# Four floats of padding between the q and k rows of an mLSTM and feed-forward kernel

## The chip, the cores and the metric

The kernel runs on one core of a Trainium2 chip. The metric is device time in microseconds for one execution, from three executions of the kernel before; lower is better. The engines are TensorE (PE, with its weight loads shown as PEld), VectorE (DVE), ScalarE (ACT), GpSimd (POOL) and SyncE (SP). SP computes nothing here; its queue issues nearly all transfers between the chip's memory (HBM) and the on-chip buffer (SBUF). Sixteen DMA engines carry them.

## The reference

There are 4 batches of 8 heads, 768 time steps, head width 40. Each of the 32 chains of (batch, head) runs an mLSTM recurrence, and its gated output feeds a feed-forward layer of 320 to 2048 to 320 with a softplus between.

```python
for t in range(S):
    m_new = np.maximum(f_gate[:, :, t] + m, i_gate[:, :, t])
    f_stab = np.exp(f_gate[:, :, t] + m - m_new)
    i_stab = np.exp(i_gate[:, :, t] - m_new)
    C = f_stab * C + i_stab * einsum('bhd,bhe->bhde', vt, kt)     # broadcast over d, e
    n = f_stab * n + i_stab * kt
    h_tilde = einsum('bhde,bhe->bhd', C, qt)
    denom = np.maximum(np.abs(einsum('bhd,bhd->bh', n, qt)), 1.0)
    y[:, :, t] = sigmoid(o_gate[:, :, t]) * h_tilde / denom
x = y.transpose(0, 2, 1, 3).reshape(B * S, H * D)                 # 3072 x 320
out = softplus(x @ w_in) @ w_out
```

## The kernel before, in words

The sequence is cut into 24 steps (one batch, 128 tokens, all 8 heads). A step `z` loads q and k of its 8 heads into one tile `qk`, and v and k by token into `vt`. It computes score products of k and q (`scores`, L463), weighs them by decays (`by_decays`), adds the part that comes from the carried state (`states`, `values`), normalises and gates the result, and writes it as columns of a tile `X`. Three steps make one `X` of 384 tokens; eight of them go through the feed-forward products: `hp` (L974, eight matmuls of 128x384 for each of 16 slices of the hidden layer) and `po` (L937, nine matmuls of 128x320 for each slice). The feed-forward weights are split into a high and a low part as they are loaded, so that the products stay exact enough.

Before the first `hp` there is a front of some 37 us: the first gates are read and scanned, three steps run one after another, and a few matmuls of the identity (`keep_warm`, L731) are placed between them. After it the feed-forward products run on PE without a break and the steps of later tiles are laid between them. The order of the work on every engine is written out: each piece of a step has a due time in a table (`WHEN`) counted in matmuls, and a context `in_order` ties each instruction to the one before it on its engine. So an instruction that waits holds up all that stands behind it on its engine, and SP is such an engine too: its loads are issued in the fixed order of the program.

A transfer also waits, ahead of its issue, for the transfer that last used its completion counter; there are eight such counters for SP, handed out in turn.

The q and k of a step lie in `qk[z.s]` in HBM as 2 halves x 40 rows (head dimension) x 2 (q, k) x 512 floats (4 heads of 128 tokens), built on the host. In SBUF each half takes 40 partitions, starting at partition 0 and 64 (`PP` is 64). Each step issues two loads `qk<-in_qk` (L382), one for each half, and one load `vt<-in_vk` (L385). The tile `qk` has three buffers.

`fc0` holds the running product of the first tokens' forget gates; it is written at L170, read by a matmul at L175 and by a small copy, all in the front. The single buffer with the tag `sig` in pool `p1` is used by the gate load of step 3 (L754) and, from step 6 on, by the tile `nw` of each step (L679).

Of the kernel before, what the change touches and what calls it, by code (L numbers as in the profile page):

```python
# [8 lines left out]
F32 = mybir.dt.float32  # L9
# [8 lines left out]
B, H, S, D = 4, 8, 768, 40  # L18
L = 128
# [4 lines left out]
HG = H // 2  # L24
# [7 lines left out]
NCHAIN = B * H  # L32
PP = 64
# [3 lines left out]
FIRST = [(1, 0), (2, 0), (0, 0), (3, 0)]  # L37
ORDER = FIRST + [(b, c) for b in range(B) for c in range(NC) if (b, c) not in FIRST]
NI = 3


@with_exitstack
def mlstm_moe_kernel(
# [11 lines left out]
    nc = tc.nc  # L55
# [7 lines left out]
    cpool = ctx.enter_context(tc.tile_pool(name="cpool", bufs=1))  # L63
    p1 = ctx.enter_context(tc.tile_pool(name="p1", bufs=1))
    p2 = ctx.enter_context(tc.tile_pool(name="p2", bufs=2))
# [30 lines left out]
    fc_d = dpool.tile([NC, NCHAIN, L], F32, name="fc_d")  # L96
    fl_d = [dpool.tile([2, 2, B, 2, NI, NQ], F32, name=f"fl_d{k}") for k in range(2)]
    flast = [cpool.tile([128, 2, B, 2, NI, NQ], F32, name=f"flast{k}") for k in range(2)]
    fl_s = cpool.tile([NCHAIN, NC, NQ], F32, name="fl_s")
    gT = cpool.tile([128, NC, NQ, B, HG], F32, name="gT")  # L100
    fcT = cpool.tile([128, NI, B, H], F32, name="fcT")
    y1z = cpool.tile([128, 2, 4, E], F32, name="y1z")
    nc.gpsimd.memset(y1z[0:Q], 0.0)
    m_end = cpool.tile([NCHAIN, 2], F32, name="m_end")
    fc0 = cpool.tile([NCHAIN, L], F32, name="fc0")

    g0 = cpool.tile([128, 2, L], F32, name="g0")
    fg0 = g0[:, 0]
# [73 lines left out]
    def later_gates(part):  # L182

        c0, c1 = ((1, NI), (NI, NC))[part]
        n, w = c1 - c0, (c1 - c0) * L
# [28 lines left out]
        yield  # L214
        fd, p0 = fl_d[part], part * NI
        nc.sync.dma_start(
# [160 lines left out]

    def load(z):

        z.qk = p2.tile([128, 2, HG, L], F32, tag="qk", bufs=3, name=f"qk{z.n}")  # L380
        for x in range(2):
            nc.sync.dma_start(z.qk[x * PP : x * PP + D], qk[z.s, x])  # L382
        z.q, z.k = z.qk[:, 0], z.qk[:, 1]
        z.vt = p2.tile([128, VW + DM], F32, tag="vt", bufs=3, name=f"vt{z.n}")
        nc.sync.dma_start(z.vt, vk[z.s])  # L385
        z.v1 = z.vt[:, 0:VW].rearrange("p (q j e) -> p q j e", q=NQ, j=HG)
        z.kt = z.vt[:, VW:]
# [124 lines left out]
    def fl(z, q):  # L512
        return flast[z.c // NI][0 : PP + D, :, z.b, :, z.c % NI, q]

# [316 lines left out]
    def plain_step(z, times):  # L831
        spare = z.s in (1, 2)
        fs = dict(
            load=load, fb=decays, scan=decay, vi=gate_values, vw=state_values, sig=out_gate,
            ga=plain_scores, pm=by_decays, st=states, cp=keep_states, old=decay_old,
            mid=mid_state, new=new_state, gc=lambda z: values(z, z.s in SPARE_C), sum=sum_values, nrm=norm, sg=scale_gate, x=gated,
            xp=turn_x, xh=high_x, xl=low_x,
        )
        for (name, f), t in zip(fs.items(), times, strict=True):
            once(f"{name}{z.s}", t, event, name, f, z)  # L840
# [3 lines left out]
    def wide_step(z, base, after):  # L844
        d = 18 + 30 * (z.s == NH)
        g = after - base
        for name, f, t in (
            ("fb", decays, -64), ("load", load, -48), ("scan", decay, -8), ("vw", state_values, 2), ("old", decay_old, 6),
            ("ga", group, 14), ("pm", by_decays, 17), ("cp", keep_states, 17), ("vi", gate_values, 20), ("mid", mid_state, 24),
            ("new", new_state, 30), ("fc", load_decays, g - 34),  # L850
        ) + ((("gc", values_wide, g),) if z.s == NS - 1 else ()) + (
            ("ym", scale_wide, g + 5), ("ya", add_wide, g + 5), ("yd", write_wide, g + 8), ("rd", read_wide, g + 42),
            ("fin", finish_wide, g + 91 + d), ("end", end_wide, g + 92 + d), ("xh", high_wide, g + 95 + d),
            ("xl", low_wide, g + 98 + d),
        ):
            once(f"{name}{z.s}" if z.s < 9 else name, base + t, event, name, f, z, base=base)
# [328 lines left out]
```

## Time and profile before

| | |
|---|---|
| Median of 3 runs | 438.4 us (436.66, 438.4, 439.52) |
| Profiled execution | span 438.4 us; the page gives no other time for it |
| PE busy | 427.3 us, 97% of the span |
| DVE, ACT, POOL busy | 253.6, 214.5, 106.1 us |
| Mean granted TensorE clock | 0.977 of full |
| Moved by DMA | 55.93 MB, mean 128 GB/s |
| Loads of q and k | 48, of 160 KB each |

A span is the time from the first to the last instruction of the core. An engine is busy when it executes, so 97% on PE says that little of the span is left without PE work, and the places where PE stands idle are the ones to look for. The granted clock is 1.0 at 2.4 GHz and 0.5 at 1.2 GHz; stretches at 0.5 lie in the first 36 us. DMA share is the mean busy share of the 16 DMA engines.

### The profile page before, as it was taken

How to read it: one execution, taken by the hardware profiler on the slowest of the kernel's cores; microseconds unless marked ns; L12 is line 12 of the kernel's file. 1: busy time of each engine (PE TensorE's matmuls, PEld its weight loads, DVE VectorE, ACT ScalarE, POOL GpSimd, SP SyncE). 2: the span in 40 equal slices, each digit the busy share in tenths (PEclk: the TensorE clock that was granted, in tenths of full speed). 3: DMA queues.
4: the chain of work that ended last, by engine and by line, in shares of the span. 5: the costliest groups of instructions: out<-in, count | busy, mean ns of one | idle time of the engine just before them, and what ended most of it. 6: DMA issues, size and time to landing. Idle time of an engine off the chain costs nothing.

```text
span 438.4 us, 12718 instructions
## 1 busy us (share of the span) xinstructions
PE 427.3 (97%) x5302; PEld 414.3 (95%) x5302; DVE 253.6 (58%) x479; ACT 214.5 (49%) x445; POOL 106.1 (24%) x171
## 2 busy tenths in 40 slices
PE   7869999999999999999999999999999999999997
PEld 6758999999999999999999999999999999999996
DVE  6678998677866556456465556466365554422221
ACT  5388898768347333534236333544336333333332
POOL 3425334545454302111132202121122200000000
PEclk9568999999999999999999999999999999999999
DMA  7877886776376373544463263553553331001001
GB/s 197 263 218 206 234 256 178 222 197 182 82 171 182 95 192 75 135 125 104 116 179 107 59 163 94 151 125 84 135 164 88 99 95 36 0 1 46 1 0 46
DMA packets 52089, 55.93 MB, mean 128 GB/s; under 512 B 5664, under 2 KB 42176, under 8 KB 52032
## 3 DMA queue, kind: packets, MB, share of 16 engines
q1 hardware_dynamic: 49008, 51.68, 43.1%
q10 hardware_dynamic: 3024, 3.44, 2.3%
q8 instruction: 41, 0.67, 0.6%
q14 instruction: 16, 0.13, 0.1%
HBM read 46.47 MB, written 8.64 MB: 126 GB/s over the span
## 4 chain that ended last, share of the span: by engine, by line
PE 95%; DMA 3%; issue 1%; ACT 0%; DVE 0%; SPq 0%
PE hp L974 41%; PE po L937 40%; PE ga L463 3%; PE gc L652 2%; PE gc L640 2%; PE ga L480 2%; PE po L731 2%; DMA qk<-in_qk 2%; DMA wr<-in_w_in 1%; PE xp L709 1%; PE gc L579 1%; PE gc L587 1%; PE xp L707 1%; PE gb L463 1%; PE gb L480 0%
## 5 line engine op out<-in xcount | busy, mean ns | idle before, releaser
L974 PE MATMUL hp<-X,wih 128*128 128x384 f32 x768 | 175.3, 337 | 0.0
L862 ACT ACTIVATE gh<-hp 128x384 fp32r<-128x384 f32 x128 | 63.0, 492 | 168.0 <-PE hp L974 140.6
L866 DVE TENSOR_TENSOR gl<-hp,gh 128x384 fp32r<-128x384 f32 x128 | 70.7, 555 | 123.1 <-ACT hp L863 122.8
L974 PEld LDWEIGHTS hp<-X,wih 128*128 128x128 f32 x768 | 133.3, 188 | 0.3 <-issue 0.2
L937 PE MATMUL po<-woh,gl 128*128 128x320 f32 x384 | 83.2, 313 | 0.0
L937 PE MATMUL po<-woh,gh 128*128 128x320 f32 x384 | 80.7, 310 | 0.0
L937 PE MATMUL po<-wol,gh 128*128 128x320 f32 x384 | 80.7, 310 | 0.0
L937 PEld LDWEIGHTS po<-woh,gh 128*128 128x128 f32 x384 | 65.8, 188 | 0.2
L974 PE MATMUL hp<-X,wil 128*128 128x384 f32 x256 | 65.7, 337 | 0.0
L937 PEld LDWEIGHTS po<-woh,gl 128*128 128x128 f32 x384 | 62.3, 188 | 0.9 <-issue 0.2
L937 PEld LDWEIGHTS po<-wol,gh 128*128 128x128 f32 x384 | 62.1, 188 | 0.8 <-issue 0.3
L863 ACT ACTIVATE hp<-hp 128x384 f32<-128x384 f32 x128 | 62.4, 487 | 0.0
L974 PEld LDWEIGHTS hp<-X,wil 128*128 128x128 f32 x256 | 46.1, 188 | 0.1
L426 POOL TENSOR_TENSOR vw<-vt,gw 128x328 f32<-128x328 f32 x22 | 17.4, 790 | 118.4 <-DVE gw L417 105.3
L412 DVE TENSOR_TENSOR_SCAN pw<-fb,ident 128x512 f32<-128x512 f32 x24 | 30.1, 1256 | 0.0
L426 POOL TENSOR_TENSOR values_in<-vt,gT 128x328 f32<-128x328 f32 x18 | 13.3, 739 | 67.7 <-PE gc L652 63.9
L463 PEld LDWEIGHTS ga<-qk 40*64 40x64 f32 x448 | 13.2, 134 | 5.5 <-issue 3.9
L558 POOL TENSOR_TENSOR c<-c,cp 104x164 f32<-104x164 f32 x20 | 14.1, 703 | 15.0 <-DVE c L426 13.7
L463 PE MATMUL ga<-qk 40*64 40x64 f32 x448 | 16.6, 224 | 1.1 <-DMA qk<-in_qk 1.1
L685 DVE RECIPROCAL nm<-nm 128x128 f32<-128x128 f32 x18 | 17.2, 953 | 0.6
L480 PE MATMUL ga<-vw,vt 64*40 64x41 f32 (+1 forms) x416 | 14.2, 222 | 2.3 <-issue 2.3
L426 POOL TENSOR_TENSOR c<-c,flast 104x164 f32<-104x164 f32 x33 | 15.6, 473 | 1.0
(159 smaller groups left out, 477.6 us busy)
## 6 DMA issues: line engine op xcount, KB each, us to landing
vt<-in_vk SPq DMA_DIRECT2D x24, 324.0 KB
qk<-in_qk SPq DMA_DIRECT2D x48, 160.0 KB
fb<-fz_d SPq DMA_DIRECT2D x42, 128.0 KB
wo<-in_w_out SPq DMA_DIRECT2D x8, 640.0 KB
wr<-in_w_in SPq DMA_DIRECT2D x8, 512.0 KB
eg<-in_oT SPq DMA_DIRECT2D x6, 576.0 KB
yd<-y SPq DMA_DIRECT2D x36, 96.0 KB
out<-ob ACTq DMA_DIRECT2D x21, 160.0 KB
```

The source lines that it names most:

```text
L412: nc.vector.tensor_tensor_scan(z.pw.rearrange(flat), z.fb.rearrange(flat), ident4.rearrange(flat), 0.0, ALU.mult, ALU.add)
L426: e.tensor_tensor(to, of, by.unsqueeze(3).broadcast_to([to.shape[0], a, b, w]), op=ALU.mult)
L463: nc.tensor.matmul(z.ga[x][y * Q : (y + 1) * Q, (i * NQ + q) * Q : (i * NQ + q + 1) * Q], z.k[rows, g, ts], z.q[rows, g, ts], start=True, ...
L480: nc.tensor.matmul(z.ga[y][x * PP : x * PP + w, c0 : c0 + E], z.kt[y * Q : (y + 1) * Q, j * D : j * D + w], z.vw[y * Q : (y + 1) * Q, q, x ...
L558: nc.gpsimd.tensor_tensor(heads(c), heads(c), z.cp[:, :, 1], op=ALU.add)
L640: nc.tensor.matmul(gc[out, x, c0 : c0 + Q], (z.cm if q else z.old)[rows, g * E : g * E + w], z.q[rows, g, q * Q : (q + 1) * Q], start=True ...
L685: nc.vector.reciprocal(nm, nm)
L862: nc.scalar.activation(gh, hp, AF.Softplus)
L863: nc.scalar.activation(hp, hp, AF.Softplus)
L866: nc.vector.tensor_tensor(gl, hp, gh, op=ALU.subtract)
L937: nc.tensor.matmul(po[j], a[:, j * 128 : (j + 1) * 128], w[:, f, :], start=(first and left[j] == 2), stop=(last and left[j] == 0),)
L974: nc.tensor.matmul(hp, a, r, start=(i == 0), stop=(i == len(seq) - 1))
```

## The change

The tile `qk` gets four more floats behind the 512 of q and behind the 512 of k in each partition, and the load writes 512 of each 516. The array that the host hands over holds the same bytes in the same order. Because of the gap a row of q and the row of k behind it no longer lie next to each other in SBUF, so that a load that was 40 pieces of 4096 bytes is now 80 pieces of 2048 bytes. The views `z.q` and `z.k` hide the gap from all that reads them. The three buffers of `qk` grow by 32 bytes per partition each. `fc0`, 512 bytes per partition, moves from a place of its own into the buffer with the tag `sig`.

```diff
+QP = 4
...
-    fc0 = cpool.tile([NCHAIN, L], F32, name="fc0")
+    fc0 = p1.tile([NCHAIN, L], F32, tag="sig", name="fc0")
...
-        z.qk = p2.tile([128, 2, HG, L], F32, tag="qk", bufs=3, name=f"qk{z.n}")
+        z.qk = p2.tile([128, 2, HG * L + QP], F32, tag="qk", bufs=3, name=f"qk{z.n}")
         for x in range(2):
-            nc.sync.dma_start(z.qk[x * PP : x * PP + D], qk[z.s, x])
-        z.q, z.k = z.qk[:, 0], z.qk[:, 1]
+            nc.sync.dma_start(z.qk[x * PP : x * PP + D, :, 0 : HG * L], qk[z.s, x])
+        z.q, z.k = (z.qk[:, i, 0 : HG * L].rearrange("p (j t) -> p j t", t=L) for i in range(2))
...
-        [np.stack([by_bits(a, b, c).transpose(2, 4, 1, 0, 3).reshape(2, D, HG, L) for a in (q, k)], axis=2) for b, c in ORDER]
+        [np.stack([by_bits(a, b, c).transpose(2, 4, 1, 0, 3).reshape(2, D, HG * L) for a in (q, k)], axis=2) for b, c in ORDER]
```

No instruction changes its place on any engine. On SP's queue the loads of the first steps stood so before (a number, the line, the operation, what is written and read, its shape, and how many follow each other):

```order
6 L382 DMA qk_0_166<-in_qk 40x1024 x2
7 L385 DMA vt_0_169<-in_vk 128x648
8 L382 DMA qk_0_230<-in_qk 40x1024 x2
9 L385 DMA vt_0_233<-in_vk 128x648
10 L737 DMA og<-in_o 128x320 x3
11 L382 DMA qk_0_292<-in_qk 40x1024 x2
```

and stand so now:

```order
6 L383 DMA qk_0_166<-in_qk 40x2x512 x2
7 L386 DMA vt_0_169<-in_vk 128x648
8 L383 DMA qk_0_230<-in_qk 40x2x512 x2
9 L386 DMA vt_0_233<-in_vk 128x648
10 L738 DMA og<-in_o 128x320 x3
11 L383 DMA qk_0_292<-in_qk 40x2x512 x2
```

The order is the same row for row; the shape of what a load writes has become three-dimensional, while the HBM side of a load is one unbroken run of 160 KB as before.

## Rows read from the trace of the kernel before

**Rows 1.** The page: busy us of each engine; granted clock in 40 slices.
```profile
PE 427.3 (97%) x5302; PEld 414.3 (95%) x5302; DVE 253.6 (58%) x479; ACT 214.5 (49%) x445; POOL 106.1 (24%) x171
...
PEclk9568999999999999999999999999999999999999
```

**Rows 2.** PE's waits: for whom, us in total, times, longest.
```profile
PE ga L480 <- issue: 2.3, 1, 2.3
...
PE po L463 <- DMA qk<-in_qk: 1.2, 2, 0.8
PE ga L463 <- DMA qk<-in_qk: 1.1, 2, 0.7
```

**Rows 3.** The chain that ended last, first 48 us: start, us, what.
```profile
1.63 4.13 DMA wr<-in_w_in
...
5.77 6.94 DMA qk<-in_qk
...
12.75 0.99 PE po L463 x25
...
24.97 2.35 issue
```

**Rows 4.** Stretches: length, busy us (instructions) by engine, clock, DMA share, GB/s.
```profile
5.27:12.09 6.82, 5.16 (x93) 4.11 (x92) 5.74 (x14) 3.19 (x5) 3.38 (x4) 1.00 0.93 240
12.09:22.33 10.24, 9.30 (x147) 8.40 (x150) 6.28 (x12) 3.52 (x5) 4.22 (x6) 0.50 0.84 269
22.33:25.75 3.42, 2.08 (x108) 1.82 (x101) 1.08 (x3) 2.88 (x11) 0.81 (x1) 1.00 1.00 336
25.75:35.99 10.24, 8.07 (x104) 6.22 (x106) 9.09 (x21) 9.12 (x14) 4.95 (x6) 0.50 0.57 155
35.99:46.23 10.24, 10.24 (x191) 9.12 (x189) 8.67 (x20) 7.75 (x15) 3.27 (x5) 1.00 0.82 250
46.23:350.00 303.77, 303.74 (x4070) 296.61 (x4071) 192.31 (x353) 155.35 (x326) 87.41 (x133) 1.00 0.52 142
```

**Rows 5.** SP's queue in order of time: start us, us, issue of which transfer, count.
```profile
3.96 0.74 SPq L382 DMA_DIRECT2D qk<-in_qk  x2
4.74 0.36 SPq L385 DMA_DIRECT2D vt<-in_vk  x1
5.14 0.91 SPq L382 DMA_DIRECT2D qk<-in_qk  x2
```

**Rows 6.** Issues on SP by tile: ns min/median/max, first and last start us.
```profile
L382 SPq DMA_DIRECT2D qk<-in_qk x48: 282/326/602, 4.0 to 337.4; - x48
...
L283 SPq DMA_DIRECT2D wr<-in_w_in x8: 373/395/552, 1.6 to 76.3; - x8
...
L671 SPq DMA_DIRECT2D yd<-y x36: 548/580/627, 102.8 to 358.8; - x36
```

**Rows 7.** Shorter stretches, columns as in group 4.
```profile
3.50:4.50 1.00, 1.00 (x7) 1.00 (x6) 0.90 (x5) 0.09 (x1) 0.00 (x0) 1.00 0.93 341
...
6.50:11.00 4.50, 3.41 (x74) 2.90 (x70) 3.53 (x6) 2.56 (x4) 2.29 (x3) 1.00 1.00 271
11.00:12.50 1.50, 0.55 (x7) 0.19 (x2) 1.50 (x3) 0.30 (x1) 1.50 (x2) 0.86 0.77 207
339.20:339.60 0.40, 0.40 (x5) 0.40 (x4) 0.36 (x2) 0.31 (x1) 0.00 (x0) 1.00 0.58 236
```

**Rows 8.** Late loads of q, k and of vt on SP's queue, as group 5.
```profile
336.82 0.85 SPq L382 DMA_DIRECT2D qk<-in_qk  x2
337.73 1.20 SPq L385 DMA_DIRECT2D vt<-in_vk  x1
```

**Rows 9.** Last reader of fc0, and first later user of its new buffer.
```profile
7.70 0.40 PE L175 MATMUL po<-ident,fc 32*128 32x32 f32 x2
...
43.08 0.32 SPq L754 DMA_DIRECT2D sig<-sgp  x1
```

## The prediction

> **What bounds the kernel now.** I read the page first: PE is busy 427.3 us of a span of 438.4 us [rows 1]. What matters is where the other 11 us lie. The stretches answer that: from 46.23 to 350 us PE is busy 303.74 us of 303.77 [rows 4], so in that stretch a load of q and k, early or late, never held PE up. The reader is to see in PE's list of waits that the loads of q and k show in it with four waits of 1.2 + 1.1 = 2.3 us together [rows 2], and in the chain of waits where they are: the chain goes from a load of the first weights (1.63 us, for 4.13 us) to a load of q and k (5.77 us, for 6.94 us), which ends at 12.71 us and lets the scores of the second step start at 12.75 us [rows 3]. From there the chain runs through PE, with one stop of 2.35 us in the third step, up to the products that fill the rest. So the change can act on the time through one thing above all: **when the second step's q and k land, at 12.71 us**. PE takes its work in a fixed order, so a shift of that landing moves everything behind it, to the end.
>
> The front has a second property. The clock that PE was granted was 1.00 (2.4 GHz) until 12.09, 0.50 (1.2 GHz) until 22.33, 1.00 until 25.75, 0.50 until 35.99 and 1.00 from then on to 350 [rows 4]. It fell at 12.09 after a stretch in which PE was busy 5.16 of 6.82 us, and again at 25.75 after 2.08 of 3.42 us. The first of these stretches is the one in which PE waits for q and k.
>
> **How many engines carry a load.** The hope that lies in 80 pieces is that they divide by 16 where 40 do not. What a load has now can be read late in the run, where few transfers meet: two loads of q and k are issued from 336.82 to 337.67 and the load of vt behind them at 337.73 [rows 8]. In the 0.4 us from 339.20 the 16 engines are busy 0.58 of the time and move 236 GB/s [rows 7]. 0.58 x 16 is 9.3 engines: the stretch looks like ten engines with work and six without. Early on the same shows: from 6.50 to 11.00 the share is 1.00, then from 11.00 to 12.50, while PE waits for the last q and k, it is 0.77 [rows 7].
>
> Will 80 pieces use all 16? In SBUF a load still fills 40 partitions, now with two pieces in each; I take it that the engines are dealt out by partitions and stay ten. The Trainium skill says this too ("DMA: Bandwidth & Descriptors", section on why a DMA increments its semaphore by 16): for each side it looks at the slowest dimension that is not 1 and takes the largest number up to 16 that divides both. For 40 on both sides that gives 10, which the shares above bear out; for 40 in SBUF and 80 in HBM it gives 10 again. By that rule the change would not reach its end; had it said 16, the sum below would end 0.8 us lower.
>
> **The sum, part by part.**
> - *Issue.* SP takes 326 ns (median of 48, the shortest 282) to issue a load of q and k [rows 6]. The new shape is not in the trace. Two rows are near: the weights `wr`, two pieces in each of 128 partitions and cut alike on both sides, 395 ns; and the write of `yd`, where 48 partitions with 4 pieces each stand against 192 pieces in HBM, 580 ns [rows 6]. Bounds: 0.07 us more a load and 0.25 us more. I take 0.25, because the new load too is cut differently on its two sides (40 by 2 against one run). Below nothing is excluded, since no row of a divided load is under 373 ns.
> - *What of it reaches 12.71.* Before the load that counts stand the two of step 0, `vt`, and the first half of step 1 [rows 5]. They start at 3.96, 4.74 and 5.14 us. With 580 ns each: 3.96 + 0.58 + 0.05 + 0.58 + 0.04 + 0.36 + 0.04 = 5.61 for the first half of step 1, which ends at 6.19, and 6.23 for the second half. Before it was issued at 5.77, the moment the weights' load landed [rows 3], so it starts 0.46 us late and its issue ends 6.81 instead of 6.05 (5.14 + 0.91), 0.76 us late. With 395 ns each it comes out at 5.68, before 5.77, and only its own 0.07 is left. Of the 0.76 us some is hidden: from 6.50 on the engines have a backlog (share 1.00), and a load that is handed over later just waits less. The least is 0, the most 0.76; I take 0.35, somewhat under half, because only the ten engines that carry q and k have to keep their backlog.
> - *Transfer.* A piece of 2048 bytes may cost more per byte than one of 4096. From 3.50 to 4.50 the 2048-byte rows of the weights move at 341 GB/s with share 0.93: 341 / (0.93 x 16) = 22.9 GB/s for a busy engine. The q and k rows: 236 / (0.58 x 16) = 25.4. Ten engines carry 16 KB each of a 160 KB load: 163,840 / 10 = 16,384 bytes, 0.645 us at 25.4 and 0.715 at 22.9, 0.07 us more a load; four loads must land by 12.71, so 0 to 0.28 us. The rows of the weights are in a mixed stretch, so I take half, 0.15.
> - *The other 44 loads.* Each holds SP 0.25 us longer, half a microsecond a step. That is covered by PE's full stretch, in which it idles 0.03 us in 304 [rows 4]; if the cover went, a step would lose at most that half microsecond where q and k gate it.
> - *`fc0` in another's buffer.* It is read last at 7.70 us, and the next user of the buffer is loaded at 43.08 us [rows 9], 35 us later: nothing. The gap itself is never read, and the matmuls read as many elements as before from a k that starts 16 bytes later; I cost that at nothing, which PE's rows of the scores (L463) will show.
>
> Sum: 438.4 + 0.35 + 0.15 = **438.9 us**. It stands against the profiled execution's span of 438.4 us, which is also the median of the three runs (436.66 to 439.52); the page shows nothing around the span. A difference within 1%, 4.4 us, is about what a measurement of this kernel can tell from none.
>
> **Rivals.**
> 1. *The issue costs no more than the cheap row* (395 ns). Then 0.07 + 0.15 remain: 438.6 us. For it: `wr` too has two pieces in a partition. Against: its two sides are cut alike.
> 2. *Sixteen engines after all.* A load then takes 5 pieces on each, 10,240 bytes at 22.9 GB/s, 0.447 us instead of 0.645: 0.2 us for each of four loads, 0.8 us off 12.71, and the issue's 0.35 on: 438.4 - 0.8 + 0.35 = 438.0 us. For it: 80 divides by 16, and the HBM side is one run. Against: the 40 partitions.
> 3. *The clock holds.* If q and k come early enough that PE's 2.3 us of waiting close up, the clock may not fall at 12.09. The stretch to 22.33 held 9.30 us of PE work at 0.50; at full clock half of it, 4.65 us, goes: 433.8 us. It needs rival 2 to be true and then some; 0.8 us of 2.3 is hardly enough.
> 4. *The clock stays low longer* (the other side). If the front's delay makes PE emptier before 35.99, where 8.07 of 10.24 us were busy, the low stretch goes on over 35.99 to 46.23, in which PE has not a gap [rows 4]. Those 10.24 us then do half of their work, and 5.1 us are added: 438.9 + 5.1 = 444.0 us. A lighter form, the full stretch of 3.42 us lost with its 2.08 us of PE work, adds 2.1: 441.0. It decides whether the later loads open a new gap in PE ahead of 35.99; for it: two falls of the clock after stretches with gaps. Against: a shift of the whole chain by half a microsecond leaves the gaps as they are.
> 5. *SP falls behind in the full stretch*, and a tile `X` comes late to its products. At half a microsecond a step for 20 steps 10 us at the most, if nothing absorbs it: 449. Against: nothing there waits now.
>
> **How the numbers follow.** Chances: the forecast 0.60, rival 1 0.14, rival 2 0.10, rival 3 0.04, rival 4 0.09 (a third of it the lighter form), rival 5 0.03. Under 434.0 us is only rival 3, and 0.01 for what I have not seen: faster by over 1% 0.05. Over 442.8 are the heavier form of rival 4 and half of rival 5: 0.06 + 0.02, and 0.01 for what I have not seen: 0.09. The same: 0.86. The range takes in the lowest run before with rival 2's 0.4 off, 436.66 - 0.4 = 436.3, and the highest run with the largest issue and transfer terms and the lighter clock form in part, 439.52 + 0.76 + 0.28 + 1.2 = 441.8. The likeliest case alone would go from 437.2 to 440.5.
>
> **What the profile after would show.** The issue row of `qk<-in_qk` with a median near 580 ns (rival 1: near 395). In a stretch with q and k alone a share that stays near 0.6 (rival 2: near 0.9). The chain's load of q and k ending near 13.2 us instead of 12.71, and the four PE waits for q and k at 2.3 us or a little more. PE's stretch from 46 to 350 us as full as before. I am wrong if the waits for q and k go, if the clock's falls move by a whole stretch, or if PE has new gaps after 46 us.

## The result: 0.64% slower, and the profile after

The changed kernel takes 440.85 us (median of 20 runs, 437.73 to 443.42) against 437.62 us for the kernel before (20 runs): ratio 1.0064, 95% interval 1.0039 to 1.0089, so 2.8 us slower (1.7 to 3.9); the two medians themselves lie 3.2 us apart. That is inside the 1% called "the same" in the prediction, and 440.85 lies in its range of 436.3 to 441.8. But the interval does not hold 1.0011, which is what the forecast of 438.9 on 438.4 comes to, and most of the time was lost in places that the prediction had costed at nothing. The profiled execution of the change has a span of 440.9 us (its time is 442.8), that of before 438.4.

The page after, first the busy time of each engine, then the granted clock in 40 slices; both answer to [rows 1].

```profile
PE 428.5 (97%) x5302; PEld 415.3 (94%) x5302; DVE 253.1 (57%) x479; ACT 214.3 (49%) x445; POOL 106.1 (24%) x171
...
PEclk9568999999999999999999999999999999999999
...
q1 hardware_dynamic: 50928, 51.68, 40.9%
```

PE does the same 5,302 matmuls, and in this execution the clock takes the same course digit for digit. The last row is the DMA queue of the loads, with its packets: 50,928 where before had 49,008, which is 1,920 more, or 48 loads times 40 additional pieces. The change did what it says.

Issue times on SP after, grouped by tile (ns min/median/max), which answer to [rows 6]:

```profile
L383 SPq DMA_DIRECT2D qk<-in_qk x48: 764/832/1193, 4.0 to 340.1; - x48
...
L386 SPq DMA_DIRECT2D vt<-in_vk x24: 391/465/478, 5.8 to 341.3; - x24
```

The issue of a q,k load takes 832 ns, where before had 326 and the upper bound of the prediction was 580. The load of `vt`, which nobody edited, takes 465 instead of 352 when it stands behind such a load. SP's queue shows it at once; this is its start, in order of time, as in [rows 5], then some rows up to 54 us:

```profile
3.98 1.79 SPq L383 DMA_DIRECT2D qk<-in_qk  x2
5.81 0.47 SPq L386 DMA_DIRECT2D vt<-in_vk  x1
6.33 1.59 SPq L383 DMA_DIRECT2D qk<-in_qk  x2
...
33.24 1.69 SPq L383 DMA_DIRECT2D qk<-in_qk  x2
...
39.39 1.19 SPq L220 DMA_DIRECT2D fc_d<-d  x1
...
46.98 0.54 SPq L210 DMA_DIRECT2D fz_d<-gt  x1
47.57 1.71 SPq L383 DMA_DIRECT2D qk<-in_qk  x2
...
51.66 1.12 SPq L284 DMA_DIRECT2D wr<-in_w_in  x1
52.83 1.16 SPq L287 DMA_DIRECT2D wr<-in_w_in  x2
54.03 1.27 SPq L405 DMA_DIRECT2D fb<-fz_d  x2
```

The two loads of step 1 are issued from 6.33 to 7.92 us, against 5.14 to 6.05 before. Yet the chain of waits has that load land where it did:

```profile
7.16 5.54 DMA qk<-in_qk
...
25.00 2.35 issue
```

7.16 + 5.54 = 12.70 us, against 12.71 [rows 3]. Issued 1.39 us later than the 5.77 there, it takes 1.4 us less to land, and the stop of 2.35 us after it stands unchanged.

Stretches after, columns as in [rows 4]. The second is one in which almost nothing but q and k moves.

```profile
6.50:11.00 4.50, 3.25 (x73) 2.84 (x68) 4.35 (x7) 2.72 (x4) 2.34 (x3) 1.00 0.83 228
340.90:341.50 0.60, 0.60 (x6) 0.60 (x5) 0.57 (x2) 0.55 (x2) 0.00 (x0) 1.00 0.64 179
46.23:350.00 303.77, 302.50 (x3960) 295.14 (x3958) 189.51 (x349) 154.52 (x323) 87.59 (x132) 1.00 0.50 143
```

0.64 x 16 is ten engines: 80 pieces are still carried by ten. The completion counters in the traces say the same: behind each of the 48 issues the counter is raised ten times as pieces land, before and after. From 6.50 to 11.00 the engines are busy 0.83 of the time and no longer 1.00 [rows 7]. And the stretch that had 0.03 us of idle PE in 304 [rows 4] now has 1.27. PE's waits name most of it (for whom, us in total, times, longest), to be read against [rows 2]:

```profile
PE ga L464 <- DMA qk<-in_qk: 1.2, 1, 1.2
PE po L464 <- DMA qk<-in_qk: 1.2, 2, 0.9
PE ga L464 <- issue: 0.9, 1, 0.9
...
PE gc L580 <- POOL c L550: 0.3, 1, 0.3
```

The waits for q and k are 2.4 us instead of 2.3. New are 0.9 us ahead of a batch of scores and 0.3 us ahead of a batch of products with the carried state (`gc`, L580). What stands behind them, the first called "issue", is seen when VectorE and ScalarE are followed in the same microseconds (timeline after; the wait ahead of an instruction stands in brackets):

```profile
60.15 1.22 DVE L413 TENSOR_TENSOR_SCAN pw<-fb,ident 128x512 f32<-128x512 f32 x1 [1.12 <-DMA fb<-fz_d]
...
61.50 0.49 DVE L427 TENSOR_TENSOR y<-gc,fcT 128x328 f32<-128x328 f32 x1
...
61.94 0.78 ACT L254 ACTIVATE mago<-wo 128x640 f32<-128x640 f32 x1 [1.27 <-DMA wo<-in_w_out]
...
62.03 0.50 DVE L609 TENSOR_TENSOR yy<-gc,y 128x328 f32<-128x328 f32 x1
...
62.63 0.69 PE L464 MATMUL ga<-qk 40*64 40x64 f32 x32 [0.86 <-issue]
```

The same work in the timeline of before, with rows of SP's queue that answer to those above:

```profile
33.22 0.69 SPq L382 DMA_DIRECT2D qk<-in_qk  x2
...
39.31 0.47 SPq L219 DMA_DIRECT2D fc_d<-d  x1
...
46.05 0.93 SPq L382 DMA_DIRECT2D qk<-in_qk  x2
...
51.20 1.63 SPq L404 DMA_DIRECT2D fb<-fz_d  x2
...
58.90 1.22 DVE L412 TENSOR_TENSOR_SCAN pw<-fb,ident 128x512 f32<-128x512 f32 x1
...
60.24 0.49 DVE L426 TENSOR_TENSOR y<-gc,fcT 128x328 f32<-128x328 f32 x1
...
60.52 0.78 ACT L253 ACTIVATE mago<-wo 128x640 f32<-128x640 f32 x1
...
60.77 0.50 DVE L608 TENSOR_TENSOR yy<-gc,y 128x328 f32<-128x328 f32 x1
...
61.63 0.69 PE L463 MATMUL ga<-qk 40*64 40x64 f32 x32
```

The reader is to see two loads that come late, and a chain from each. SP, level with before to 0.1 us at 33.24 and at 39.39 us, hands over the decays of step 5 (`fb`) at 54.03 instead of 51.20. Of these 2.8 us the step's own pair of q,k loads makes 0.78 (1.71 for 0.93), two single long issues 0.72 each (`fc_d` 1.19 for 0.47, `wr` 1.12 for 0.40), and the other 0.6 us is spread over several.

The first chain: VectorE's scan of the decays, which waited for nothing before, now waits 1.12 us. VectorE works in order, so `y` and `yy` of step 4, which stand behind the scan and have nothing to do with it, are 1.26 us late. TensorE's scores start 0.10 us after `yy`, which reads step 4's PSUM tile `gc`, has ended (62.53). (In all five traces with this stop the scores start 0.11 us after `yy`; where there is no stop, 0.32 to 0.39 us.) That start is 1.00 us later than before.

The second chain: the load behind the decays, of the feed-forward weights `wo`, is handed over at 55.40 instead of 52.93 us. ScalarE's `mago`, which waited for nothing here before, now waits 1.27 us for it, and what stands behind it on ScalarE is late too. Two more delays of TensorE follow, 0.27 us ahead of `xp` and 0.5 us ahead of `gc` (the wait for POOL), when the starts of equal matmuls are compared; slow_issue_vt below has these two without the first. In sum that makes 1.8 us.

The remaining 0.7 us is not in any wait. From 84 us on PE is full in both kernels, and still falls behind little by little. PE's matmuls by tile after (ns min/median/max, first and last start; `gb` is first used at the scores near 84 us):

```profile
L464 PE MATMUL gb<-qk x288: 218/218/267, 84.2 to 350.4; 40*64 40x64 f32 x144
...
L938 PE MATMUL po<-woh,gl x384: 302/308/421, 46.2 to 437.3; 128*128 128x320 f32 x192
```

The same two rows of before:

```profile
L463 PE MATMUL gb<-qk x288: 218/218/268, 82.3 to 348.1; 40*64 40x64 f32 x144
...
L937 PE MATMUL po<-woh,gl x384: 304/309/416, 46.1 to 434.8; 128*128 128x320 f32 x192
```

437.3 - 84.2 = 353.1 us after, and 434.8 - 82.3 = 352.5 before.

### The profile page after: what moved, and what is told of

It reads as the page before. It is cut to its first block, busy times and chain, and to the rows that moved or that the text cites. A ratio compares the mean times of both kernels' runs of the same rounds, so it can differ in the third digit from the quotient of the medians.

```text
span 440.9 us, 12718 instructions
## 1 busy us (share of the span) xinstructions
PE 428.5 (97%) x5302; PEld 415.3 (94%) x5302; DVE 253.1 (57%) x479; ACT 214.3 (49%) x445; POOL 106.1 (24%) x171
## 3 DMA queue, kind: packets, MB, share of 16 engines
q1 hardware_dynamic: 50928, 51.68, 40.9%
## 4 chain that ended last, share of the span: by engine, by line
PE 94%; SPq 1%; DMA 1%; issue 1%; ACT 1%; POOL 1%; DVE 0%; POOLq 0%
PE hp L975 40%; PE po L938 39%; PE ga L464 3%; PE gc L653 2%; PE gc L641 2%; PE ga L481 2%; PE po L732 2%; DMA qk<-in_qk 1%; PE gc L580 1%; SPq L383 1%; PE gc L588 1%; PE xp L710 1%; PE gb L464 1%; PE xp L708 0%; PE gb L481 0%
## 5 line engine op out<-in xcount | busy, mean ns | idle before, releaser
L938 PE MATMUL po<-woh,gl 128*128 128x320 f32 x384 | 82.8, 311 | 0.0
L559 POOL TENSOR_TENSOR c<-c,cp 104x164 f32<-104x164 f32 x20 | 14.0, 701 | 15.0 <-DVE c L427 13.7
L550 POOL TENSOR_TENSOR c<-c,cp 104x164 f32<-104x164 f32 x20 | 13.7, 686 | 9.0 <-ACT cp L763 7.3
```

What stands on the lines that cost most here:

```text
L550: nc.gpsimd.tensor_tensor(heads(z.cm), heads(z.cm), z.cp[:, :, 0], op=ALU.add)
L559: nc.gpsimd.tensor_tensor(heads(c), heads(c), z.cp[:, :, 1], op=ALU.add)
L938: nc.tensor.matmul(po[j], a[:, j * 128 : (j + 1) * 128], w[:, f, :], start=(first and left[j] == 2), stop=(last and left[j] == 0),)
```

## Experiments

The length of the front, up to the first product in TensorE, differs from one execution to the next: 33.6 to 38.3 us over the 14 traces, as the half-clock stretches of [rows 4] fall differently, in two executions of one kernel too (the change 37.36 and 35.79). The seven traces with a slow issue have the shorter fronts on the mean, 35.7 us against 37.2 in the six with a quick issue and 40 rows. The timing of many runs does not show such a gain for the change: it loses 2.8 us (1.7 to 3.9), of which the marks below find 2.5 behind the front. The spread is larger than the effect, so single times and spans tell little here. I therefore read three marks in each trace: A, the start of the first product (`hp`); B, the start of the 1,100th matmul, one of the scores near 79 to 84 us; C, the start of the last product. "Landed" is the last piece of step 5's decays, counted from A. All in us, the issue in ns.

```
kernel             issue  landed   A to B   B to C   A to C less before   ratio of times
before               326   19.9    45.15    352.33     0
the change           832   22.8    46.94    353.03    +2.5    1.0064 [1.0039, 1.0089]
after_again          832   22.7    46.88    353.05    +2.4    -
slow_issue           775   23.2    46.99    352.23    +1.7    1.0017 [0.9988, 1.0047]
slow_issue_again     775   22.9    46.78    352.33    +1.6    -
slow_issue_vt        774   21.6    45.97    352.25    +0.7    -
layout_only          333   21.4    45.25    353.03    +0.8    1.0031 [1.0000, 1.0061]
decays_first         826   early   45.19    353.06    +0.8    1.0029 [0.9999, 1.0058]
fc0_only             328   20.0    45.17    352.24    -0.1    -
cut_alike            356   20.1    45.19    353.58    +1.3    1.0000 [0.9968, 1.0031]
cut_alike_no_pad     346   21.3    45.18    352.25     0.0    1.0015 [0.9986, 1.0045]
rows_48              421   20.6    45.26    353.41    +1.2    1.0031 [0.9997, 1.0066]
pad_of_16            832   22.6    46.26    352.43    +1.2    -
alike_pad_of_16      356   21.0    45.20    352.38    +0.1    0.9989 [0.9958, 1.0020]
```

Two theories came out of the comparison: **the slow issue** (theory A in the texts below) makes SP late with step 5's decays, which shows between A and B; **the shifted buffers** (theory C: three wider tiles and `fc0` moved, so that the buffers behind the three of q and k lie 416 bytes lower) slow some matmuls, which shows between B and C. Rivals to both: the 2048-byte pieces cost transfer time (theory B); or `fc0` in the other buffer does it.

**layout_only**: the buffers of the change, but the gap behind k, so that a load has 40 pieces of 4096 bytes again.

```diff
-        z.qk = p2.tile([128, 2, HG * L + QP], F32, tag="qk", bufs=3, ...)
+        z.qk = p2.tile([128, 2 * (HG * L + QP)], F32, tag="qk", bufs=3, ...)
-            nc.sync.dma_start(z.qk[x * PP : x * PP + D, :, 0 : HG * L], qk[z.s, x])
+            nc.sync.dma_start(z.qk[x * PP : x * PP + D, 0 : 2 * HG * L], qk[z.s, x].rearrange("p i w -> p (i w)"))
```

> The buffer is as large as in the change and fc0 is moved as there, but the padding lies behind k, so that a load stays 40 pieces of 4096 bytes. Theory A (SP: issuing a load takes 0.83 us instead of 0.33, SP falls behind, and the decays of step 5 and a weights load come late): issue near 326 ns, no stop of PE after 46 us, the time of the kernel before, 437.6 us within 0.4%. Theory B (80 pieces move more slowly): also as before. Theory C (other addresses of the buffers, or fc0 in another's buffer): as the change, some 0.6% slower, 440.5 us.

By tile, the issue and the two PE rows as for the change:

```profile
L383 SPq DMA_DIRECT2D qk<-in_qk x48: 281/333/1387, 4.0 to 336.9; - x48
...
L464 PE MATMUL gb<-qk x288: 218/218/267, 81.4 to 347.7; 40*64 40x64 f32 x144
...
L938 PE MATMUL po<-woh,gl x384: 306/308/421, 45.2 to 434.6; 128*128 128x320 f32 x192
```

The issue is back at 333 ns and A to B at 45.25, but 434.6 - 81.4 = 353.2: the creeping loss stays, without a divided load. The timing (1.0000 to 1.0061) can't tell a part of the loss from all of it.

**cut_alike**: the change, with q and k apart in HBM (`np.stack` along axis 1: in each half first the rows of q, then those of k), so that both sides of the load are cut 40 by 2 by 512.

```diff
-            nc.sync.dma_start(z.qk[x * PP : x * PP + D, :, 0 : HG * L], qk[z.s, x])
+            nc.sync.dma_start(z.qk[x * PP : x * PP + D, :, 0 : HG * L], qk[z.s, x].rearrange("i p w -> p i w"))
...
-        [np.stack([...], axis=2) for b, c in ORDER]
+        [np.stack([...], axis=1) for b, c in ORDER]
```

> As the change, 80 pieces of 2048 bytes into the padded buffer, but q and k lie apart in HBM (host layout half, q or k, row), so that both sides of a load are cut alike, 40 by 2 by 512. Theory A: the issue falls to some 400 ns, as the weights' load that is cut alike, and with it the loss goes: as before within 0.4%, PE without a stop after 46 us. Theory B: 80 pieces all the same, so 0.6% slower as the change. Theory C: 0.6% slower too.

There are still 80 pieces of 2048 bytes, yet the issue is 356 ns and A to B 45.19. So it is not the number of pieces that costs SP its time but that the two sides were cut differently. B to C is 353.58; the 0.5 us above layout_only all arise at 98.4 to 98.7 us, in two delays of 0.44 and 0.10 us ahead of `hp`, where PE waits for VectorE's `gl`. The timing (0.9968 to 1.0031) has neither this nor the 0.7 us of the buffers clear of noise.

**slow_issue**: the kernel before, every byte in its old place, with the q,k loads built without the short form of issue. In the built program a transfer carries a mark when its issue was prepared as the program was built; that is called the short form here. The q,k loads of before and of cut_alike carry it and those of the change do not, which is why I tried it. Of the prediction's two near rows, the 395 ns of `wr` carry it and the 580 ns of `yd` do not.

```diff
+            nc.dge_precook = False
             nc.sync.dma_start(z.qk[x * PP : x * PP + D], qk[z.s, x])
+            nc.dge_precook = True
```

> The kernel before with its 40 pieces of 4096 bytes, its buffers and its order, but the q and k loads are built without the short form of issue. Theory A: their issue takes longer than 326 ns, and if it comes to 0.8 us the decays of step 5 land late and the time is that of the change, 0.6% slower; if it comes to 0.58 us only (the other long issues), SP is late by half as much at that place, some 1.4 us of 2.8, and the loss is 0.2% or none. Theories B and C: no loss, 437.6 us.

Of four views, its issue by tile, the new wait among PE's, the scan in VectorE's timeline, and the load of step 1 in the chain:

```profile
L383 SPq DMA_DIRECT2D qk<-in_qk x48: 716/775/1395, 4.0 to 337.6; - x48
```
```profile
PE ga L465 <- issue: 1.3, 1, 1.3
```
```profile
58.64 1.23 DVE L414 TENSOR_TENSOR_SCAN pw<-fb,ident 128x512 f32<-128x512 f32 x1 [1.50 <-DMA fb<-fz_d]
```
```profile
6.93 5.06 DMA qk<-in_qk
```

The slow issue alone, with 40 pieces and no gap, brings the stops: 1.8 us between A and B, nothing between B and C. And step 1's q and k land at 11.99 us, earlier than the 12.71 of before. The timing by itself (1.0017, interval over 1) tells neither theory from the other; the stretches do.

**decays_first**: the change, with the decays of step 5 taken to the front of the program's order.

```diff
-        ... 'gc4': 81.333, 'fb5': 81.667, ...
+        ... 'gc4': 81.333, 'fb5': 16.8, ...
```

> The change, with one thing moved on SP's queue: the load of step 5's decays is issued ahead of step 5's q and k and no longer eleven loads behind. Theory A: the scan of step 5 no longer waits, the stop of 0.86 us before step 5's scores goes, and 0.8 to 1.8 us come back (0.2 to 0.4%), 439 to 440 us; what is left hangs on the weights load that is late behind it. Theories B and C: it stays 0.6% slower, 440.5 us.

The issue stays slow (826 ns), and the stops are gone: A to B 45.19, and PE has no wait behind A. So it is at this place of SP's queue that the slow issue reaches PE. The edit does not tell the two chains apart: with `fb5` out of the way the load of `wo` behind it is issued 16.9 instead of 18.0 us after A too, and lands at 23.4 instead of 24.6, where ScalarE wants it at 23.2. B to C is 353.06, untouched.

**fc0_only**: before, with `fc0` in the buffer of `sig` and nothing else, which moves the steps' buffers by 512 bytes.

```diff
-    fc0 = cpool.tile([NCHAIN, L], F32, name="fc0")
+    fc0 = p1.tile([NCHAIN, L], F32, tag="sig", name="fc0")
```

> The kernel before with fc0 moved into the buffer with the tag sig and nothing else: the large buffers lie 512 bytes lower, with no padding. It asks where the 0.7 us come from that all three kernels with the changed buffers lost behind the 1,100th matmul (352.33 us before, 353.03 to 353.06 with them, beside a stop of PE in one). If any shift of the buffers does it: 353.0 us there. If it is the shift by 416 bytes that the padding makes of it: 352.3 us. In both cases no stop of PE before step 5's scores, 45.2 us from the first hp matmul to the 1,100th.

45.17 and 352.24: nothing, as the prediction had it.

**cut_alike_no_pad**: before, with only the order in HBM of cut_alike. No gap, no buffer moved, but a partition takes two pieces of 2048 bytes.

```diff
-            nc.sync.dma_start(z.qk[x * PP : x * PP + D], qk[z.s, x])
+            nc.sync.dma_start(z.qk[x * PP : x * PP + D], qk[z.s, x].rearrange("i p j t -> p i j t"))
```

> The kernel before with its buffers, but q and k apart in HBM, so that a load has 80 pieces of 2048 bytes cut alike on both sides, without padding and with fc0 in its place. Theory A: issue near 356 ns, no stop of PE, 45.2 us to the 1,100th matmul and 352.3 us behind it: the time of the kernel before within 0.3%. Theory B: slower by the pieces, 0.6%.

45.18 and 352.25: the 80 pieces by themselves cost nothing. A piece of 2048 bytes takes 84 ns (median behind 300 us, in every kernel with such pieces), one of 4096 bytes 159 ns (in every kernel with 40 of them). Eight of the one against four of the other are 672 and 636 ns on each of ten engines: 0.04 us a load.

**rows_48**: before, loading 48 rows instead of 40 (the first 8 once more, which nobody reads).

```diff
-            nc.sync.dma_start(z.qk[x * PP : x * PP + D], qk[z.s, x])
+            nc.sync.dma_start(z.qk[x * PP : x * PP + DR], qk[z.s, x])
...
+    qk = np.concatenate([qk, qk[:, :, 0 : DR - D]], axis=2)
```

> The kernel before with each load widened from 40 to 48 rows (the eight more are never read; 20% more bytes), in pieces of 4096 bytes. If the engines are dealt out by rows, 48 rows go to 16 engines with 3 pieces each where 40 go to 10 with 4; a stretch with q and k alone shows a share near 0.9 and not 0.6, and the load of step 1 lands about 0.5 us before 12.7. Issue stays near 326 ns and nothing after 46 us changes. If so, up to 0.5 us less than before (0.1%), which the timing will hardly tell; if the engines stay ten, five pieces each, as before or 0.3 us slower.

A stretch with little but q and k, and then the chain's load of step 1:

```profile
337.40:338.20 0.80, 0.80 (x7) 0.80 (x6) 0.77 (x2) 0.59 (x2) 0.00 (x0) 1.00 1.07 305
```
```profile
5.84 6.38 DMA qk<-in_qk
```

This is what sixteen engines look like: a share of 1.07 where ten give 0.6, 305 GB/s, and a completion counter that is raised sixteen times as pieces land. A piece of 4096 bytes takes 218 ns here instead of 159 (medians behind 300 us), so that three on each of sixteen engines are 0.65 us and four on each of ten 0.64: late in the run a load is not carried faster, but it carries a fifth more. The issue did not stay near 326 ns as expected; it takes 421. The load lands at 12.22, half a microsecond earlier than before. That need not be the engines' doing, since with ten engines and a slow issue it landed at 11.99 to 12.70. No gain shows in the time (1.0031); B to C holds a stop of 1.11 us at 95.8 us, without which it would be 352.30. Half a microsecond is less than this timing can tell, so what an earlier landing is worth stays open. That it is worth much is not borne out.

**slow_issue_vt**: slow_issue, with the load of `vt` built in the same way, to double the dose.

> The kernel before with its buffers and pieces, with q, k and vt all issued without the short form: a third more of the suspected cost in each step. Theory A: vt too takes some 0.8 us to issue, SP comes another 0.4 us later for each step, the stop before step 5's scores grows from 1.3 to about 2 us, and the stretch from the first hp matmul to the 1,100th goes from 46.99 to some 47.8 us. Theories B and C: 45.2 us.

A miss. The issue of `vt` is 0.52 us, where slow_issue had 0.46 already without this edit, so the dose hardly grew, and A to B was 45.97, less than in slow_issue. The decays landed at 21.6 us from A, just when the scan wants them (21.6 in all the traces where it does not wait), and the scan did not wait. What is left came by the second chain alone, as ScalarE's timeline has it:

```profile
57.24 0.79 ACT L253 ACTIVATE mago<-wo 128x640 f32<-128x640 f32 x1 [0.32 <-DMA wo<-in_w_out]
```

Behind it `xp` came 0.23 us and `gc` 0.53 us late, as in the change. More delay on SP in sum does not mean more at this place.

**after_again** and **slow_issue_again**: the same kernels once more, since the dose had missed.

> The changed kernel once more, with nothing edited, to see how much of the stop of TensorE behind step 4 belongs to one execution. Theory of the slow issue: an issue of a q,k load again takes 0.76 to 0.84 us; the decays of step 5 are handed over at least 1.5 us later after the first products than before (13.9 us there), and TensorE stops for 0 to 1.5 us between 59 and 70 us, more only if they come after 16.2 us. Theory of the shifted buffers: from TensorE's 1,100th matmul to the last again 353.0 us within 0.1, since addresses do not change from one execution to the next. Rival (the first profile was an accident): issues near 0.33 us, 352.3 us behind the 1,100th matmul.

> The kernel before with its q,k loads built without the short form of issue, once more, nothing edited. Theory of the slow issue: 0.7 to 0.9 us an issue, the decays of step 5 handed over 1.5 to 4.5 us later after the first products than before (13.9 us), and stops of TensorE of 0 to 2 us between 59 and 70 us; behind the 1,100th matmul 352.2 us within 0.1, since no buffer is shifted. Rival (the stop in the first look came from something else): decays as late, and no stop although they come after 16.5 us.

VectorE's scan in slow_issue_again (timeline):

```profile
59.49 1.23 DVE L414 TENSOR_TENSOR_SCAN pw<-fb,ident 128x512 f32<-128x512 f32 x1 [1.21 <-DMA fb<-fz_d]
```

The stops came back in both, 1.73 and 1.63 us between A and B, and so did the 353.05 of the change and the 352.33 without moved buffers. The decays were handed over 15.6 us after A in after_again, earlier than the 16.2 that I had given as the point from which the stop exceeds 1.5 us; they still landed too late, and the stops made 1.73. What decides for the first chain is the landing: 19.9 to 21.4 in the seven traces with a quick issue and `fb5` in its place, none of which stops there; 22.6 to 23.2 in five with a slow one, all of which do, and 21.6 in slow_issue_vt, on the edge. On the mean of each group the second half of the decays is handed over 15.4 us after A (14.6 to 16.5) and 17.0 (16.1 to 18.5), and lands at 20.6 and 22.6; the transit in between is 4.8 to 6.4 and 4.6 to 6.5 us. So the slow issue makes the landing 2.0 us later on the mean, 1.6 of it by the hand-over. The step's own pair gives 0.8 of that and its `vt` 0.1. Whence the other half comes stays open: step 4's pair, 1.0 us longer, was made up for in SP's idle time by 39 us in the change, and long single issues fall on both groups.

**pad_of_16** and **alike_pad_of_16**: the change and cut_alike, each with a gap of 16 elements. The buffers behind the three of q and k then lie 128 bytes lower than before instead of 416. (`gh` and `gl`, which `po` reads, are among them; the weights and `X` lie 512 bytes lower in all these kernels, and in fc0_only, too.)

```diff
-QP = 4
+QP = 16
```

> The change with a gap of 16 elements (64 bytes) instead of 4. Every buffer behind the three of q and k then lies 128 bytes lower than before, not 416. Theory of the shifted buffers: it is the odd shift that lengthens the interval of some matmuls, so from the 1,100th matmul to the last it takes 352.25 us within 0.1, as before, and not 353.03; the intervals of po from wol and gh go back to those of before. The issue of a q,k load stays at 0.76 to 0.84 us, and a stop between 59 and 70 us of 0 to 2 us may stay. Rival (any move of these buffers, or the gap between q and k itself, costs it): 353.0 us.

> The change with both its costs taken out and its layout kept: q and k beside each other in a row of HBM cut as the tile is (80 pieces of 2048 bytes on both sides), and a gap of 16 elements. Theory of slow issue and shifted buffers: issue near 0.35 us, no stop of 0.5 us or more behind step 4, 352.25 us within 0.1 behind the 1,100th matmul; the time is that of before, ratio 0.997 to 1.003. Rival (the padding costs by the pieces or by the gap): 353.0 us or more behind the 1,100th matmul, ratio 1.003 to 1.008.

Of alike_pad_of_16, by tile, the issue and the two PE rows:

```profile
L383 SPq DMA_DIRECT2D qk<-in_qk x48: 288/356/1546, 4.0 to 337.8; - x48
...
L464 PE MATMUL gb<-qk x288: 218/218/268, 82.8 to 348.6; 40*64 40x64 f32 x144
...
L938 PE MATMUL po<-woh,gl x384: 303/308/416, 46.6 to 435.3; 128*128 128x320 f32 x192
```

435.3 - 82.8 = 352.5, as before: a gap and moved buffers cost next to nothing here when the move is 128 bytes (352.38 and 352.43 in the table, 0.1 us above before and just outside what was expected). With both costs out, the padded kernel takes the time of the one before (0.9989, interval 0.9958 to 1.0020). pad_of_16 has lost the creep too and kept stops of 1.1 us in sum between A and B. One part of its expectation missed: the start-to-start interval of `po` from `wol` and `gh` stayed long, and others became shorter instead (last section).

## Why the prediction was right, and where it was wrong

**Right: the engines.** Ten carry the load, by the share of 0.64 and the ten landings after, and sixteen look like rows_48. By the rule of the Trainium skill ("DMA: Bandwidth & Descriptors", section on why a DMA increments its semaphore by 16), 40 against 80 gives 10 and 48 against 48 gives 16; the traces agree with both. Rival 2's price, 0.2 us less for a load on sixteen engines, had taken each engine at the same speed; rows_48, where a piece takes 218 ns instead of 159, does not bear that out.

**Right: the transfer is small, and `fc0` costs nothing; the loss needs no move of the clock.** A load's pieces take 0.04 us more, within the 0 to 0.07 of the working. The waits for q and k are 2.4 us where 2.3 or a little more was forecast. Rival 1 fell with the issue and rival 2 with the ten engines. The clock's course is the same in the two profiled executions, but that alone does not exclude rivals 3 and 4: it differs between executions of one kernel (in after_again the clock is at half from 14.04 to 20.87 us and from 27.69 to 34.52). But the time behind the front accounts for the loss without them.

**Wrong: the size of the issue.** The term was 0.25 us more a load at the most, from the write of `yd` (580 ns); it measured 832 - 326 = 0.51 us, twice as much. The step that failed is "two rows are near": the write is a different shape in the other direction, and what other shapes cost is no upper bound for a shape the trace does not show.

**Wrong: what of it reaches 12.71.** The sum put 0.35 us of issue and 0.15 us of transfer into this landing and had them move the whole chain. With twice the issue, nothing arrived: 12.70 us, and in six more traces with a slow issue 12.0 to 12.6, where the six with a quick issue and 40 rows have 12.57 to 12.78. So the sign of the term is in doubt, not only its size. The share from 6.50 to 11.00, which fell from 1.00 to 0.83, fits a simple reading: a slower SP hands over the competing loads later too, and the q and k that are on their way find the engines emptier. That was not tested by itself.

**Wrong: the other 44 loads cost nothing.** This is the step that cost most of the time. "Covered by PE's full stretch, in which it idles 0.03 us in 304" was read as slack, but a PE that does not wait shows only that nothing came late, not by how much it came early. The decays of step 5 were 1.7 us early in the profiled execution (landed 19.9, wanted 21.6 after A), and in others with a quick issue 0.2 to 1.6; `wo` behind them was 1.8 us early (landed 21.5, wanted 23.2). In the change they landed 2.9 and 3.1 us later, of which long single issues made a part. Rival 5 (SP falls behind in the full stretch, 0.03) was the mechanism, though with other tiles than it named, `fb` and `wo` and not `X`, and at one place, not in 20 steps: 1.8 us, where the working allowed a step half a microsecond. What spoke against it, "nothing there waits now", was no argument against it. slow_issue brings the stops alone, and decays_first takes them away: that the slow issue does it, and at this place of SP's queue, is shown. How the 1.8 us divide between the two loads is read from the timelines.

**Wrong: the k that starts 16 bytes later.** The gap itself does cost nothing, but the three wider tiles push the buffers behind them, and that costs 0.7 us between B and C: shown by layout_only (it comes without the divided load), fc0_only (a pure 512 bytes do nothing) and pad_of_16 (128 bytes do nothing). The term was put at nothing because the change was followed only in the instructions that it touches, not in the addresses of all others.

**The sum by what was measured**: 1.8 (stops) + 0.7 (addresses) = 2.5 us, where the profiled spans differ by 440.9 - 438.4 = 2.5 (their fronts happened to be alike: A at 37.30 and 37.36 us) and the ratio of the timed runs stands for 2.8 (1.7 to 3.9). slow_issue's 1.6 to 1.7 and layout_only's 0.8, measured apart, make 2.4 to 2.5 as well. The direction came out as forecast, and the time within its range, for reasons that the forecast did not give: its 0.5 us at 12.71 was not there, and 2.5 us elsewhere were. So much of it was luck.

## What to carry to other kernels

An engine that never waits is not one with slack: before an issuing queue is made slower, take for each transfer behind the edit the time between its landing and its first use, and compare it with the delay that the edit can bring to that place, on top of the microsecond or two by which it varies anyway. Cut both sides of a load alike; here that, and not the number or size of the pieces, decided whether its issue took 0.35 or 0.83 us. When a tile grows, look where the tiles behind it come to lie, and measure more than one width of the gap: moves of 128 and 512 bytes cost 0.1 us or less here, and one of 416 cost 0.7 us.

## What had not been expected of the hardware

- **The price of an issue depends more on its form than on its pieces.** 40 pieces: 326 to 333 ns in the short form, 775 ns without it. 80 pieces: 346 to 356 ns cut alike, 832 ns cut differently. Pieces or engines are not free either: 48 pieces on sixteen engines took 421 ns in the short form.
- **The addresses of SBUF buffers change how fast full-rate matmuls follow each other.** From 100 to 435 us, start-to-start, with 416 bytes: `po` from `wol` and `gh` 147.4 to 150.1 ns (336 intervals, +0.91 us), `hp` from `wih` +0.37, `po` from `woh` with `gh` -0.30 and with `gl` -0.26. With 128 bytes: +0.73, -0.13, -0.35 and -0.12, which nearly cancel. The sums are the same to 0.1 us in every execution with the same addresses. What in the addresses decides stays open; `hp` slows although the buffers that it reads lie as in fc0_only, which lost nothing.
- **Single issues of 1 to 2.5 us** stand in every trace, 6 to 11 of them, some near the same times in most (83, 118, 241 and 290 us), others at changing places (after: 1.12 us at 51.66, for a load that takes 0.40 as a rule). Together with 4.6 to 6.5 us of transit they set how much of the slack is left in a given execution.
